# A two-layer mixture-of-experts kernel behind a scan: w1 copies of the units past the scan move to VectorE, router logits stay on the chip, one more weight staging buffer, zeroing spread over steps, and a lighter early weight schedule

## The chip, the core and the metric

The kernel runs on one core of a Trainium2 chip. The metric is the device time of one launch in microseconds (us); lower is better. TensorE (PE) multiplies matrices, VectorE (DVE), ScalarE (ACT) and GpSimd (POOL) do the elementwise work, and SyncE (SP) issues most of the transfers, in program order on one queue. GpSimd issues the transfers whose target rows come from an index list (scatters).

## The reference

`x` and `f_logit` have shape (4, 5056, 256). A gated recurrence runs along the sequence, and its output, 20224 rows of 256, goes through two mixture-of-experts layers with 8 experts each (256 to 1024 to 256). The first layer is applied only to rows with a positive skip score and adds its result to the row; the second is applied to all rows and replaces them.

```python
f = lower_bound + (1 - lower_bound) * sigmoid(f_logit)
h = f[:, t] * h + (1 - f[:, t]) * x[:, t]        # for every t; y[:, t] = h

# layer 1 (rows with x @ w_skip > 0), layer 2 (all rows, without the "x +")
e = argmax(x @ w_gate); g = softmax(x @ w_gate)[e]
out = x + g * (relu(x @ w1[e]) @ w2[e])
```

## The kernel before, in words

**Regions.** DRAM holds a buffer `regions` with one stretch of rows for each expert of each layer. A row that has been routed is scattered to the end of its expert's stretch (row of 256 numbers, 8 logits of the second layer, token number, gate; `W` = 272 floats, 1088 bytes). A *unit* is 256 rows (or 128, for what is left over) of one expert, read back as one block.

**Steps.** Units have numbers u = 0 to 125. A unit has four steps; step k = 4u + f. In step k, `Moe.step` first stores what the unit before has finished (`put1`), then issues the first product of quarter f (`mm1`, line 604: 12 matmuls, so 48 for a unit), then the work ahead (`ahead`): at f = 3 the load of unit u + 2 (`load`, line 559), at f = 0 the copy of w1 for unit u + 1 (`stage`, lines 568 to 578), at f = 2 the transposes of unit u + 1 (`xpose`, line 591). Then follows the second product of the step two before (`mm2`, lines 632 to 634), the end of a unit (`finish1` or `finish2`), and the side work (`side`). The order of the instructions on every engine is the order of this text.

**Stages.** Sixteen iterations of the scan run before step 0, with the splitting of the first layer's weights into two float16 halves (`weights`, `wload`, `wsplit`; 4 quarters for each of 8 experts, 32 calls in all; `WI`, `WS` and `WD` say in which steps of which iteration a call is made). Units 0 to 27 run beside the rest of the scan, one iteration (512 rows) for each unit. Units 28 to 41 are the rest of layer 1: 28 to 31 and 32, 34, 36, 38, 40, 41 have 256 rows, 33, 35, 37, 39 have 128. Units 42 to 125 are layer 2, the last six of 128 rows. Units 0 to 7 and 42 to 49 have a known expert and read w1 in place in the weight store `wt`. For the others the expert is only known on the chip, and 1024 KB of w1 are copied to a fixed place: in layer 1 by a transfer on SP's queue (line 575, `wt<-wt` for units 8 to 27, `w1s<-wt` for 28 to 41), in layer 2 by a VectorE copy (line 578).

**From layer 1 to layer 2.** Finished layer-1 rows can't be scattered at once, since their places depend on counts. `put1` writes a unit's rows to a DRAM buffer `mid` (line 651) and their logits, 32 bytes for each row, to a DRAM buffer `midl` (line 653). After the scan, three sorts (`sort_later`, `sorting`; 52, 12 and 16 tiles of 128 rows) read the logits back (line 1258) and compute target rows and gates on VectorE. Then `sort_some` sends one pair of tiles for each step: SP reads it from `mid` into one of 7 or 8 slots in the weight store (line 1336), three steps later ScalarE writes the gates (line 1327) and GpSimd scatters the two tiles (line 272). The third sort starts at step 172. The lists of layer 2 are made from step 4 * 42 + 12 = 180 on; they are needed by the load of unit 50 in step 195.

**Buffers.** Blocks of rows have three buffers, so the load of unit u + 2 waits until what unit u - 1 stored has landed. The staging buffers `wst` (two) take the quarters of the second layer's weights (`weights2`: each call first splits the quarter of two calls ago, then loads the next, lines 1127 and 1130) and, once, a block of zeros `zr2`, which `zero2` writes behind the last row of each expert of layer 2: 8 transfers (lines 783 to 785), issued by the list generator, of which `listing` takes up to 5 pieces in one step.

Of the kernel before, what the change touches and what calls it, by code (L numbers as in the profile page):

```python
# [8 lines left out]
F32 = mybir.dt.float32  # L9
# [8 lines left out]
P = 128  # L18
B, S, D, E, F = 4, 5056, 256, 8, 1024
NT = B * S  # L20
# [5 lines left out]
UT = 256  # L26
UJ = UT // P
CP = NT + 2 * UT
NREG = 2 * E
LR = E // 2 * CP + UT  # L30
# [4 lines left out]
I0, LN, NEARLY, K1A, K1B = 16, 4, 8, 6, 4  # L35
K2E, K2A, K2B = 8, 70, 6
NFIX = E // LN
NMID = LN * NEARLY * UJ + K1A * UJ + K1B
GC = GT // CJ


DL, DB, UF, KL = 2, 3, 5, 12

WQ = [(e, k) for e in range(E) for k in (2, 3)] + [(e, k) for e in range(E) for k in (0, 1)]
WI, WS, WD = [1, 2] * 8, [1, 3], 1
WL = 17
WT = 24
LG, LB, LA1 = 4, 3, 1
# [10 lines left out]
CLG, CTOK, CGATE = D, D + E, D + E + 1  # L59
# [33 lines left out]
def moe_chain(ctx: ExitStack, tc: tile.TileContext, xT, fT, lb, wg, w1a, w2a, w1b, w2b, out):  # L93
    nc = tc.nc
# [4 lines left out]
    regf = reg[:]  # L99
# [188 lines left out]
    lists = ctx.enter_context(tc.tile_pool(name="lists", bufs=1))  # L288

    midt = tc.dram_tile([NMID * P, W], F32, name="mid")  # L290
    mid = midt[:]
    midl = tc.dram_tile([P, NMID, E], F32, name="midl")[:]
    vals = lists.tile([P, NMID], F32, name="vals")

    def region(name):
# [239 lines left out]
    class Moe:  # L535


        def __init__(m, pools, w1s):
            m.w1s = w1s
            m.xp, m.hp, m.px, m.pm, m.po, m.pr = pools  # L540
            m.t, m.put = {}, None

# [23 lines left out]
        def stage(m, u):  # L566

            t = m.t[u]
            if t.lo == t.hi:
                t.w1 = wt[:, t.lo : t.lo + W2O]  # L570
                return
            t.w1 = m.w1s(u)
            if not t.L.l2:
                o = nc.sync.value_load(t.L.reg[0:1, 1, t.ur], min_val=t.lo, max_val=t.hi)
                nc.sync.dma_start(t.w1, wt[:, bass.ds(o, W2O)])
            else:
                o = nc.vector.value_load(t.L.reg[0:1, 1, t.ur], min_val=t.lo, max_val=t.hi)
                nc.vector.tensor_copy(t.w1, wt[:, bass.ds(o, W2O)])  # L578
# [68 lines left out]

        def put1(m):
            t, m.put = m.put, None
            r0 = (t.L.tiles + t.at * t.uj) * P  # L650
            nc.sync.dma_start(mid[r0 : r0 + t.ut, :].rearrange("(j p) w -> p j w", p=P), t.rows)
            j0 = r0 // P
            nc.sync.dma_start(midl[:, j0 : j0 + t.uj, :], t.rows[:, :, CLG : CLG + E])

        def send1(m, u):

# [73 lines left out]
    with ExitStack() as ph:  # L730
# [4 lines left out]
        mp = ph.enter_context(tc.tile_pool(name="mp", bufs=2))  # L735
        hp = ph.enter_context(tc.tile_pool(name="hp", bufs=3))
        ul = ph.enter_context(tc.tile_pool(name="ul", bufs=1))
        late = K()

        def w1s1(u):  # L740

            if u < U1:
                o = E * ES + u % 2 * W2O
                return wt[:, o : o + W2O]
            return w1s2(u)
# [3 lines left out]

        U1 = nchunk + 3 - I0 + 1  # L750
        pools = (mp, hp, pt, pm, po, pr)
        moe, tail = Moe(pools, w1s1), Moe(pools, w1s2)

        ap_ = ph.enter_context(ExitStack())
        xp_ = ap_.enter_context(tc.tile_pool(name="ldx", bufs=3))
# [15 lines left out]
        def zero2(pool):  # L771

            zs = pool.tile([P, E], F32, name="zs")
            nc.vector.tensor_tensor(out=zs, in0=S2.c0, in1=sgn8, op=ALU.mult)
            yield
            at = pool.tile([1, E], I32, name="at")
            nc.vector.tensor_tensor(out=at, in0=zs[0:1, :], in1=blk8[0:1, :], op=ALU.add)
            yield
            z = late.s.tile([P, F], F32, tag="wst", name="zr2")[:, : UJ * W].rearrange("p (j w) -> p j w", w=W)
            nc.gpsimd.memset(z, 0.0)  # L780
            for e in range(E):
                r0 = e // 2 * CP + e % 2 * (CP - UT - NT)
                r = nc.sync.value_load(at[0:1, e : e + 1], min_val=r0, max_val=r0 + NT)
                dst = regf[bass.ds(r + LR, UT), :].rearrange("(j p) w -> p j w", p=P)
                r = nc.sync.dma_start(dst, z)
                for g in ("scat", "ld1", "zero"):
                    tc.declare_no_dep(r.ins, group=g, reason="rows without tokens, of one expert")
                tc.add_to_no_dep_group("zero", r.ins)
                yield

        C = {}
        Q = {}
# [432 lines left out]
        DG = K()  # L1225
        DG.todo, DG.now, DG.send, DG.held, DG.n = [], None, [], [], 0

        def sort_later(k):
            last = [None] * NMID
            for u, (L, at) in enumerate(units):  # L1230
                uj = L.ut // P
                for j in range(uj):
                    last[L.tiles + at * uj + j] = u
            a = LN * NEARLY * UJ
            t0 = max(t for t in range(a) if 4 * last[t] + 6 <= k)
            t0 += t0 % 2
            for t0, t1 in ((0, t0), (t0, a), (a, NMID)):
                DG.todo.append((t0, t1 - t0, max(last[t0:t1])))
            DG.most = max(n for _, n, _ in DG.todo)

            late.past = late.d.tile([P, P], F16, name="past")
            nc.vector.tensor_scalar(out=late.past, in0=ltri, scalar1=-1.0, scalar2=None, op0=ALU.add)

        def sorting(t0, n, c):

            v = nc.vector
            shp = [P, n, E]
            m = DG.most

            def tile3(name, dt=F32):  # L1250
                t = late.d.tile([P, m * E], dt, name=name)
                return t[:, : n * E].rearrange("p (n e) -> p n e", e=E)

            def tile1(name, dt=F32, bufs=1):
                return late.d.tile([P, m], dt, name=name, bufs=bufs)[:, :n]

            lg = tile3("b_lg")
            nc.sync.dma_start(lg, midl[:, t0 : t0 + n, :])

            on = late.d.tile([P, m * E], F16, name="b_on")[:, : n * E]  # L1260
            nc.gpsimd.memset(on, 1.0)
            nc.gpsimd.memset(on.rearrange("p (e n) -> p e n", e=E)[:, :, 0], 0.0)
            yield
            yield
            mx = tile1("b_mx")
            v.tensor_reduce(out=mx, in_=lg, op=ALU.max, axis=AX.X)
            v.tensor_tensor(out=lg, in0=lg, in1=mx.unsqueeze(2).broadcast_to(shp), op=ALU.subtract)
# [126 lines left out]
        n1 = LN * NEARLY + K1A + K1B  # L1394
        n = n1 + K2E + K2A + K2B
        q2 = iter(range(4, 4 * E + 2))

        def side(k):
# [8 lines left out]
            if s == CS:  # L1407
                e, r = divmod(i - (I0 - CK), LN)
                if r == 0 and 0 <= e < NEARLY:
                    lists_of_scan(e)  # L1410
            if s == 3 and i == nchunk + 2:
                for _ in G[2]:
                    pass
                ap_.close()
                late.w = ph.enter_context(tc.tile_pool(name="w1s", bufs=WB))
                late.s = ph.enter_context(tc.tile_pool(name="wst", bufs=2))
                late.l = ph.enter_context(tc.tile_pool(name="lists2", bufs=1))
                late.d = ph.enter_context(tc.tile_pool(name="small2", bufs=1))
                lists_after_scan()
                sort_later(k)  # L1420
# [4 lines left out]
            if k == 4 * n1 + KL:  # L1425
                assert not GL.todo and DG.counted == NMID
                lists_of_layer2()
                assert len(units) == n
            if i > nchunk + 2:
                listing(LT if k < 4 * n1 else LT2, True, 3)  # L1430
                sort_some(k)
            else:
                listing(max(GL.n, 1), s in PS, LA)
            if i < I0:
# [7 lines left out]
            u = i - I0 - n1  # L1442
# [52 lines left out]
```

## Time and profile before

| what | value |
|---|---|
| median of 3 runs | 1603.25 us (1598.87 to 1607.89) |
| the profiled execution's own time | 1619.11 us |
| its span, first to last instruction | 1617.4 us |
| PE busy | 1506.5 us (93%) |
| DVE, ACT, POOL busy | 904.6, 719.7, 499.6 us |
| mean granted TensorE clock | 0.975 |

Durations and waits come from the one profiled execution, which is 15.9 us above the median of the runs. The clock is the share of full speed (2.4 GHz) that was granted; the other level is 1.2 GHz, so 0.83 in a stretch means that it was at the lower level for a third of it. The DMA share is the mean busy share of 16 DMA engines.

### The profile page before, as it was taken

The page shows a single profiled execution, that of the slowest core. Times are in us where ns is not written, and L with a number is a line of the kernel's source. Part 1 is how long each engine was busy: PE and PEld are TensorE (multiplying, and loading weights), DVE is VectorE, ACT ScalarE, POOL GpSimd, SP SyncE. Part 2 cuts the span into 40 slices and gives each one's busy share as a digit, 9 for nine tenths or more (in the row PEclk, how much of TensorE's full clock was granted, in tenths as well). Part 3 has the DMA queues.
Part 4 walks back from the last instruction along what each step waited for, and adds up shares of the span by engine and source line. Part 5 has one row for each costly group of instructions (what it writes and reads, how often), then busy time and mean ns, then how long its engine had stood idle before and what let it go on. Part 6 is the DMA issues. An engine that isn't in the chain of part 4 may idle for free.

```text
span 1617.4 us, 41213 instructions
## 1 busy us (share of the span) xinstructions
PE 1506.5 (93%) x13897; PEld 1343.9 (83%) x13898; DVE 904.6 (56%) x1915; ACT 719.7 (44%) x1376; POOL 499.6 (31%) x509
## 2 busy tenths in 40 slices
PE   6877999999999977898899999999999999999996
PEld 5776888888887866787689999989989998998996
DVE  5887687878775633445575555544444444444443
ACT  6885667666662221333344444433333333333332
POOL 1663556454643265113311111111111111111111
PEclk9987999999999999999999999999999999999998
DMA  8876647777754689616333332211111111111110
GB/s 290 278 262 215 224 167 246 245 247 235 251 195 168 193 277 298 219 51 209 115 100 96 100 107 88 88 54 54 46 51 55 48 48 55 48 50 52 55 42 26
DMA packets 138998, 228.56 MB, mean 141 GB/s; under 512 B 24571, under 2 KB 97791, under 8 KB 134448
## 3 DMA queue, kind: packets, MB, share of 16 engines
q1 hardware_dynamic: 119600, 172.33, 33.5%
q0 software_dynamic: 19200, 53.53, 9.1%
q8 instruction: 132, 2.16, 0.6%
q14 instruction: 66, 0.54, 0.1%
HBM read 120.16 MB, written 70.86 MB: 118 GB/s over the span
## 4 chain that ended last, share of the span: by engine, by line
PE 80%; DMA 6%; DVE 5%; issue 4%; ACT 3%; SPq 1%; POOL 1%; another core or an unknown queue 1%; POOLq 0%; ACTq 0%; DVEq 0%
PE ps_m L604 36%; PE ps_o L632 12%; PE ps_o L633 12%; PE ps_o L634 12%; PE ps_x L591 3%; DVE xt L838 1%; PE ps_t L862 1%; DMA rows<-regions 1%; DMA ft<-in_fT_dram 1%; DMA wt<-mid 1%; PE ps_l L890 1%; DMA midl<-rows 1%; PE ps_v L1019 1%; DMA regions<-rw,dest 1%; ACT hh L615 1%
## 5 line engine op out<-in xcount | busy, mean ns | idle before, releaser
L616 DVE SCALAR_TENSOR_TENSOR hl<-ps_m,hh 128x512 f16<-128x512 f32 (+1 forms) x504 | 336.8, 669 | 595.5 <-ACT hh L615 574.1
L615 ACT ACTIVATE hh<-ps_m 128x512 f16<-128x512 f32 (+1 forms) x504 | 292.3, 580 | 704.2 <-PE ps_m L604 522.2
L632 PE MATMUL ps_o<-wt,hh 128*128 (+2 forms) x1936 | 532.9, 275 | 6.7 <-DVE rows L640 4.2
L634 PE MATMUL ps_o<-wt,hl 128*128 (+2 forms) x1936 | 532.5, 275 | 2.5 <-issue 2.5
L633 PE MATMUL ps_o<-wt,hh 128*128 (+2 forms) x1936 | 532.7, 275 | 0.6 <-issue 0.6
L604 PE MATMUL ps_m<-xh,w1s 128*128 128x256 f16 (+1 forms) x2880 | 509.1, 268 | 8.5 <-issue 3.6
L604 PEld LDWEIGHTS <-w1s 128*128 128x128 f16 x4320 | 407.1, 98 | 60.2 <-issue 10.6
L272 POOL DMA_INDIRECT out_dram<-rows,dest x162 | 157.8, 974 | 751.9 <-ACT rows L669 687.1
L604 PE MATMUL ps_m<-xl,w1s 128*128 128x256 f16 (+1 forms) x1440 | 379.6, 268 | 1.7 <-issue 1.4
L604 PE MATMUL ps_m<-xh,wt 128*128 128x256 f16 x1152 | 216.9, 276 | 4.6 <-issue 4.5
L633 PEld LDWEIGHTS <-hh 128*128 128x128 f16 x1936 | 190.5, 98 | 33.1 <-issue 8.6
L634 PEld LDWEIGHTS <-hl 128*128 128x128 f16 x1936 | 190.4, 98 | 27.8 <-issue 2.5
L632 PEld LDWEIGHTS <-hh 128*128 128x128 f16 x1936 | 190.5, 98 | 23.5 <-issue 0.7
L272 POOL DMA_INDIRECT regions<-rw,dest x158 | 173.3, 1097 | 84.5 <-issue 50.0
L604 PEld LDWEIGHTS <-wt 128*128 128x128 f16 x1728 | 168.4, 99 | 30.8 <-issue 10.5
L604 PE MATMUL ps_m<-xl,wt 128*128 128x256 f16 x576 | 158.8, 276 | 2.4 <-issue 2.1
L272 POOL DMA_INDIRECT regions<-wt,b_dest x80 | 78.8, 984 | 99.6 <-ACT wt L1327 58.3
L578 DVE COPY w1s<-wt 128x4096 f16 x76 | 93.3, 1228 | 8.5 <-issue 2.1
L838 DVE TENSOR_TENSOR_SCAN xt<-ft,end,xt 128x512 f32<-128x512 f32 (+4 forms) x78 | 95.0, 1248 | 0.3
L591 PE MATMUL ps_x<-ident,rows 128*128 128x128 f32 x484 | 75.3, 277 | 19.7 <-DMA rows<-regions 15.0
L593 DVE SCALAR_TENSOR_TENSOR xl<-ps_x,xh 128x512 f16<-128x512 f32 (+1 forms) x126 | 83.3, 661 | 10.0 <-ACT xh L592 9.9
L669 ACT ACTIVATE rows<-ps_o,rows 128x256 f32<-128x256 f32 x162 | 68.6, 473 | 32.7 <-PE ps_o L634 32.3
(231 smaller groups left out, 1298.8 us busy)
## 6 DMA issues: line engine op xcount, KB each, us to landing
rows<-regions SPq DMA_DIRECT2D x116, 272.0 KB
wt<-wt SPq DMA_DIRECT2D x20, 1024.0 KB
ft<-in_fT_dram SPq DMA_DIRECT2D x39, 512.0 KB
xt<-in_xT_dram SPq DMA_DIRECT2D x39, 512.0 KB
w1s<-wt SPq DMA_DIRECT2D x14, 1024.0 KB
wt<-mid SPq DMA_DIRECT2D x40, 272.0 KB
mid<-rows SPq DMA_DIRECT2D x38, 272.0 KB
wt<-in_w2a_dram SPq DMA_DIRECT2D x16, 512.0 KB
```

Of the source, the lines that this page charges most:

```text
L272: r = nc.gpsimd.indirect_dma_start(out=dst, out_offset=bass.IndirectOffsetOnAxis(ap=idx_ap, axis=0), in_=rows_ap, in_offset=None, bounds_c ...
L578: nc.vector.tensor_copy(t.w1, wt[:, bass.ds(o, W2O)])
L591: nc.tensor.transpose(ps[:, d, j * P : (j + 1) * P], t.rows[:, j, d * P : (d + 1) * P], ident)
L593: nc.vector.scalar_tensor_tensor(out=t.xl, in0=ps, scalar=SX, in1=t.xh, op0=ALU.mult, op1=ALU.subtract)
L604: nc.tensor.matmul(ps[:, f, :], lhsT=t.w1[:, wo : wo + P], rhs=x[:, d, :], start=f == 0 and k == 0, stop=f == 1 and k == 5, skip_group_che ...
L615: nc.scalar.activation(hh, ps, AF.Relu)
L616: nc.vector.scalar_tensor_tensor(out=hl, in0=ps, scalar=0.0, in1=hh, op0=ALU.max, op1=ALU.subtract)
L632: nc.tensor.matmul(ps, lhsT=hh[:, f, js], rhs=hi, start=first, stop=False)
L633: nc.tensor.matmul(ps, lhsT=hh[:, f, js], rhs=lo, start=False, stop=False)
L634: nc.tensor.matmul(ps, lhsT=hl[:, f, js], rhs=hi, start=False, stop=last)
L669: nc.scalar.activation(y, t.ps[j][:, :D], AF.Copy, scale=t.rows[:, j, CGATE : CGATE + 1])
L838: nc.vector.tensor_tensor_scan(x[:, d, s0:s1], f[:, d, s0:s1], x[:, d, s0:s1], init, ALU.mult, ALU.subtract)
```

## The change

- Layer-1 units from 28 on (`u >= U1`) copy w1 with VectorE instead of a transfer on SP's queue.
- Logits are gathered on the chip by a ScalarE copy in `put1`. For scan units they go to `midl` once for four units (256 bytes for each partition); for units 32 to 41 they stay in a tile `late.lg`, which the last sort reads in place, without a transfer and two steps sooner.
- The sorts are cut into pieces of at most `NB` = 24 tiles: 24, 24, 16 and 16 tiles instead of 52, 12 and 16.
- The staging pool `wst` gets a third buffer.
- The 8 zero transfers are put in a list, and one is issued in each step.
- The lists of layer 2 start one step earlier (`KL` 11).
- Of the 32 weight calls, 21 instead of 24 are made in the first 16 scan iterations; the others follow from iteration 16 (step 0) on instead of 17.

```diff
+NSCAN = LN * NEARLY * UJ
+NMID = NSCAN + K1A * UJ + K1B
+NB = 24
-DL, DB, UF, KL = 2, 3, 5, 12
+DL, DB, UF, KL = 2, 3, 5, 11
-WI, WS, WD = [1, 2] * 8, [1, 3], 1
+WI, WS, WD = [1, 2, 1] * 5 + [1], [1, 3], 0
...
-    midl = tc.dram_tile([P, NMID, E], F32, name="midl")[:]
+    midl = tc.dram_tile([P, NSCAN, E], F32, name="midl")[:]
+    lgs = lists.tile([P, LN * UJ, E], F32, name="lgs")
...
-            if not t.L.l2:
+            if u < m.by_dma:
                 o = nc.sync.value_load(t.L.reg[0:1, 1, t.ur], min_val=t.lo, max_val=t.hi)
                 nc.sync.dma_start(t.w1, wt[:, bass.ds(o, W2O)])
             else:
...
         def put1(m):
             t, m.put = m.put, None
+            j0 = t.L.tiles + t.at * t.uj
+            if j0 >= NSCAN:
+                nc.scalar.copy(late.lg[:, j0 - NSCAN : j0 - NSCAN + t.uj, :], t.rows[:, :, CLG : CLG + E])
+            else:
+                j = j0 % (LN * UJ)
+                nc.scalar.copy(lgs[:, j : j + t.uj, :], t.rows[:, :, CLG : CLG + E])
+                if j + t.uj == LN * UJ:
+                    nc.sync.dma_start(midl[:, j0 - j : j0 - j + LN * UJ, :], lgs)
             r0 = (t.L.tiles + t.at * t.uj) * P
             nc.sync.dma_start(mid[r0 : r0 + t.ut, :].rearrange("(j p) w -> p j w", p=P), t.rows)
-            j0 = r0 // P
-            nc.sync.dma_start(midl[:, j0 : j0 + t.uj, :], t.rows[:, :, CLG : CLG + E])
...
-        moe, tail = Moe(pools, w1s1), Moe(pools, w1s2)
+        moe, tail = Moe(pools, w1s1, U1), Moe(pools, w1s2, 0)
...
             nc.gpsimd.memset(z, 0.0)
+            yield
             for e in range(E):
-                r0 = e // 2 * CP + e % 2 * (CP - UT - NT)
-                ...
-                yield
+                ZG.append((z, at, e))
+        ZG = []
+        def zero_one():
+            if not ZG:
+                return
+            z, at, e = ZG.pop(0)
+            ...            # the same register load and transfer as before, for one expert
...
-            t0 = max(t for t in range(a) if 4 * last[t] + 6 <= k)
-            t0 += t0 % 2
-            for t0, t1 in ((0, t0), (t0, a), (a, NMID)):
+            t0 = max(t for t in range(0, NSCAN, LN * UJ) if 4 * max(last[:t], default=0) + 6 <= k)
+            cuts = sorted({*range(0, t0, NB), *range(t0, NSCAN, NB), NSCAN, NMID})
+            for t0, t1 in zip(cuts[:-1], cuts[1:]):
                 DG.todo.append((t0, t1 - t0, max(last[t0:t1])))
+            late.lg = late.d.tile([P, NMID - NSCAN, E], F32, name="lg")
...
-            lg = tile3("b_lg")
-            nc.sync.dma_start(lg, midl[:, t0 : t0 + n, :])
+            if c:
+                lg = late.lg
+            else:
+                lg = tile3("b_lg")
+                nc.sync.dma_start(lg, midl[:, t0 : t0 + n, :])
...
-            yield
-            yield
+            if not c:
+                yield
+                yield
...
-                late.s = ph.enter_context(tc.tile_pool(name="wst", bufs=2))
+                late.s = ph.enter_context(tc.tile_pool(name="wst", bufs=3))
...
                 sort_some(k)
+                zero_one()
```

## Rows read from the trace of the kernel before

**Rows 1.** Windows: stretch, length; busy PE, PEld, DVE, ACT, POOL; clock, DMA share, GB/s.
```profile
261.00:510.00 249.00, 239.44 (x2403) 212.21 (x2402) 191.72 (x489) 156.70 (x293) 125.12 (x111) 1.00 0.69 231
525.00:695.00 170.00, 146.85 (x1315) 123.52 (x1313) 78.07 (x217) 43.90 (x108) 63.03 (x68) 0.96 0.73 239
695.00:750.00 55.00, 55.00 (x506) 49.37 (x505) 25.40 (x72) 18.41 (x38) 7.64 (x16) 1.00 0.27 85
...
791.00:1567.00 776.00, 776.00 (x7105) 698.33 (x7103) 371.56 (x605) 286.80 (x521) 138.33 (x142) 1.00 0.21 66
```

**Rows 2.** Windows of line 604's matmuls alone, 48 to a unit; clock, DMA share.
```profile
525.00:572.00 47.00, 23.70 (x192) 1.00 0.66 218
572.00:673.00 101.00, 41.92 (x387) 0.93 0.82 268
673.00:695.00 22.00, 11.68 (x97) 1.00 0.48 153
...
750.00:791.00 41.00, 14.19 (x97) 0.83 0.60 197
...
1567.00:1604.00 37.00, 20.00 (x288) 1.00 0.12 37
```

**Rows 3.** Waits of SP's queue, whole run: total us, times, longest us.
```profile
SPq L559 <- DMA midl<-rows: 51.6, 29, 6.6
...
SPq L559 <- DMA mid<-rows: 16.9, 7, 5.5
```

**Rows 4.** Chain that ended last, 640 to 690: start us, us, what.
```profile
669.83 6.63 DMA midl<-rows
676.48 2.71 DMA rows<-regions
```

**Rows 5.** Waits of PE, stretch 525 to 695: total us, times, longest us.
```profile
PE ps_x L591 <- DMA rows<-regions: 6.5, 5, 2.6
PE ps_m L604 <- issue: 5.0, 9, 1.0
...
PE ps_m L604 <- DMA w1s<-wt: 2.5, 2, 1.5
```

**Rows 6.** Line 272 in the stretch 525 to 673: ns min/median/max, first and last start.
```profile
L272 POOL DMA_INDIRECT regions<-wt,b_dest x64: 968/975/978, 551.5 to 656.6; - x64
```

**Rows 7.** Timeline of SP, stretch 690 to 800: start us, us, instruction.
```profile
742.59 3.87 SPq L785 DMA_DIRECT2D regions<-zr  x4
...
749.53 5.24 SPq L785 DMA_DIRECT2D regions<-zr  x4
...
759.71 0.39 SPq L559 DMA_DIRECT2D rows<-regions  x1
```

**Rows 8.** Timelines of PE and POOL, 756 to 784; idle time before in brackets.
```profile
763.69 1.11 PE L591 MATMUL ps_x<-ident,rows 128*128 128x128 f32 x4 [7.14 <-DMA rows<-regions]
...
777.34 0.27 PE L604 MATMUL ps_m<-xl,wt 128*128 128x256 f16 x1 [1.14 <-issue]
...
762.50 0.98 POOL L272 DMA_INDIRECT regions<-wt,b_dest  x1 [0.30 <-issue]
```

**Rows 9.** Waits of SP's queue, stretch 735 to 800.
```profile
SPq L1127 <- DVE wt L183: 13.4, 2, 8.8
```

**Rows 10.** Groups by line: count, busy us, mean ns.
```profile
L578 DVE COPY w1s<-wt 128x4096 f16 x76 | 93.3, 1228 | 8.5 <-issue 2.1 <-DMA wst<-in_w1b_dram 1.2
...
L183 DVE SCALAR_TENSOR_TENSOR wt<-wt 128x1024 f16<-128x1024 f32 x24 | 29.4, 1227 | 18.1 <-ACT wt L182 16.8 <-issue 1.1
...
L920 ACT COPY lg<-ls 128x32 f32<-128x32 f32 (+1 forms) x40 | 8.7, 216 | 0.0
```

**Rows 11.** Timeline of DVE, scan before the units: one line 826 an iteration.
```profile
59.02 1.23 DVE L826 SCALAR_TENSOR_TENSOR xt<-ft,xt 128x1024 f32<-128x1024 f32 x1 [0.93 <-ACT rw L865]
...
67.36 1.22 DVE L826 SCALAR_TENSOR_TENSOR xt<-ft,xt 128x1024 f32<-128x1024 f32 x1
...
76.53 1.23 DVE L826 SCALAR_TENSOR_TENSOR xt<-ft,xt 128x1024 f32<-128x1024 f32 x1 [0.94 <-ACT ft L821]
```

More of the change, by code (lines that the diff above doesn't have):

```diff
@@ L37 @@
 NFIX = E // LN
-NMID = LN * NEARLY * UJ + K1A * UJ + K1B
+NSCAN = LN * NEARLY * UJ
+NMID = NSCAN + K1A * UJ + K1B
+NB = 24
 GC = GT // CJ
-DL, DB, UF, KL = 2, 3, 5, 12
+DL, DB, UF, KL = 2, 3, 5, 11
 WQ = [(e, k) for e in range(E) for k in (2, 3)] + [(e, k) for e in range(E) for k in (0, 1)]
-WI, WS, WD = [1, 2] * 8, [1, 3], 1
+WI, WS, WD = [1, 2, 1] * 5 + [1], [1, 3], 0
 WL = 17
@@ L291, in moe_chain @@
     mid = midt[:]
-    midl = tc.dram_tile([P, NMID, E], F32, name="midl")[:]
+    midl = tc.dram_tile([P, NSCAN, E], F32, name="midl")[:]
+    lgs = lists.tile([P, LN * UJ, E], F32, name="lgs")
+    late = K()
     vals = lists.tile([P, NMID], F32, name="vals")
@@ L535, in moe_chain, with __init__ @@
     class Moe:
-        def __init__(m, pools, w1s):
-            m.w1s = w1s
+        def __init__(m, pools, w1s, by_dma):
+            m.w1s, m.by_dma = w1s, by_dma
             m.xp, m.hp, m.px, m.pm, m.po, m.pr = pools
@@ L737, in moe_chain @@
         ul = ph.enter_context(tc.tile_pool(name="ul", bufs=1))
-        late = K()
         def w1s1(u):
@@ L780, in zero2 @@
             nc.gpsimd.memset(z, 0.0)
+            yield
             for e in range(E):
-                r0 = e // 2 * CP + e % 2 * (CP - UT - NT)
[L783 to L788, printed above, removed]
-                yield
+                ZG.append((z, at, e))
[4 more added lines that the diff above has]
+            z, at, e = ZG.pop(0)
+            r0 = e // 2 * CP + e % 2 * (CP - UT - NT)
+            r = nc.sync.value_load(at[0:1, e : e + 1], min_val=r0, max_val=r0 + NT)
+            dst = regf[bass.ds(r + LR, UT), :].rearrange("(j p) w -> p j w", p=P)
+            r = nc.sync.dma_start(dst, z)
+            for g in ("scat", "ld1", "zero"):
+                tc.declare_no_dep(r.ins, group=g, reason="rows without tokens, of one expert")
+            tc.add_to_no_dep_group("zero", r.ins)
         C = {}
@@ L1233, in sort_later @@
                     last[L.tiles + at * uj + j] = u
-            a = LN * NEARLY * UJ
-            t0 = max(t for t in range(a) if 4 * last[t] + 6 <= k)
-            t0 += t0 % 2
-            for t0, t1 in ((0, t0), (t0, a), (a, NMID)):
+            t0 = max(t for t in range(0, NSCAN, LN * UJ) if 4 * max(last[:t], default=0) + 6 <= k)
+            cuts = sorted({*range(0, t0, NB), *range(t0, NSCAN, NB), NSCAN, NMID})
+            for t0, t1 in zip(cuts[:-1], cuts[1:]):
                 DG.todo.append((t0, t1 - t0, max(last[t0:t1])))
-            DG.most = max(n for _, n, _ in DG.todo)
+            late.lg = late.d.tile([P, NMID - NSCAN, E], F32, name="lg")
             late.past = late.d.tile([P, P], F16, name="past")
@@ L1247, in sorting @@
             shp = [P, n, E]
-            m = DG.most
+            m = NB
             def tile3(name, dt=F32):
@@ L1428, in side @@
                 assert len(units) == n
+            if k == 4 * (n1 + K2E - 2) + 3:
+                assert not ZG and not DG.send and not DG.held and DG.now is None
             if i > nchunk + 2:
```

## The prediction

> **What bounds the kernel now.** I read the windows by stage first. Past 791 us TensorE is busy 776.00 of 776 us at full clock, and from 695 to 750 it is busy 55.00 of 55 [rows 1]: in layer 2 nothing but TensorE's own work sets the time, so the change can win nothing there. In the scan stage (261 to 510) TensorE is busy 239 of 249. The stage with room is 525 to 695, units 28 to 41: 147 of 170, clock 0.96, DMA share 0.73.
>
> The windows of the first product alone turn this into units [rows 2]. 673 to 695 holds 97 matmuls, two units, so a unit of 256 rows takes 10.9 us when nothing is late; 1567 to 1604 holds six units of 128 rows in 37 us, 6.2 each. Against these paces:
>
> - 525 to 572: four units in 47 us instead of 43.6, 3.4 lost.
> - 572 to 673: four large and four small units in 101 us instead of 68.4, 32.6 lost.
> - 750 to 791: two units in 41 us instead of 21.8, 19.2 lost.
>
> Then I ask what was late. In the first two stretches TensorE waits for blocks of rows (6.5 us), for w1 transfers (2.5) and for "issue", where the profile names nothing (5.0 for the first product) [rows 5]; the rest is lower clock after each wait (0.93) and waits further back. The chain of waits shows the pattern: the small transfer of logits lands 6.63 us after its issue, only then may the next block be loaded, 2.71 us more [rows 4]. SP's queue says the same over the run: 29 loads waited for logits, 7 for the rows beside them [rows 3]. In the third stretch the load of unit 48, due in step 187, goes out at 759.71, behind eight zero transfers that begin at 742.59 and end at 754.77 [rows 7] and behind a weight load that waited for a split, up to 8.8 us [rows 9]. TensorE stands 7.14 us for it, and later crawls one matmul at a time [rows 8], while GpSimd runs sixteen scatters back to back.
>
> **The change, part by part.**
>
> *Copies and logits, 525 to 695.* Fourteen transfers of 1024 KB go, with the logits' transfers of these units. In their place come fourteen VectorE copies of 1.23 us [rows 10], 17 us on an engine that is busy 78 of 170, and ScalarE copies of about 0.2 us (nearest row: 216 ns for 32 numbers a partition). A copy stands at the start of a unit, ahead of the halves that the second product needs two steps later; layer 2 runs so at full pace, large units and small [rows 1, 2], so I cost it at nothing while that cover of two steps holds.
>
> What is late next? First the row store: a load then waits for `mid` instead of `midl`. From the store to the transposes there are four steps: 10.9 us in large units, about 8.6 across a large and a small one. Before, 6.63 + 2.71 = 9.3 us had to fit. The row store is issued ahead of the logits and was seldom the last [rows 3], so it should fit, with less margin in small units. Then GpSimd: 64 scatters of 0.975 us lie between 551.5 and 656.6 [rows 6], with 0.30 between neighbours [rows 8], so they need 81.6 of these 105.1 us, and this train can shrink by 23.5 us at most. No copy lies in that stretch before the change; some nine would lie in it after. If a copy and a scatter exclude each other, the train needs 81.6 + 9 x 1.23 = 92.7 us and shrinks by 12.4.
>
> No row shows the two together. The Trainium skill (SBUF — State Buffer, Who interferes with whom) says that a VectorE copy in a two-port mode and GpSimd's work on a scatter block each other for a whole instruction; by this the term would be 12 us and not 21, and no run here shows it yet.
>
> TensorE need not follow GpSimd step by step, since seven slots stand between. Lower bound of the gain: the waits that the rows name, 6.5 + 2.5 = 9 us. Upper: 23.5 for the train, the 3.4 before it and some 3 after it, 30 us. I take 21, nearer to the train's limit, because the transfers that go are the largest in the stretch.
>
> *Zeros, third buffer, earlier last sort, 750 to 791.* One zero transfer then takes about 1 to 1.3 us of SP in a step of 2.7 us, so SP is no longer twelve microseconds behind, and a weight load does not wait until the zero block has landed. The last sort ends two steps earlier, so its scatters don't fall together with late loads; the earlier lists have the same effect. The load of unit 48 should go out near 748 us. One flaw: the zero block now keeps a buffer through eight steps (183 to 190), so the weight load of step 188 has two buffers left and still waits for a split [rows 9]; the load of unit 49 three steps later covers most of that. Lower bound: the 7.14 us wait plus about 1 us of low clock, 8; upper: 19.2. I take 17, with the crawl gone, since it stands beside the bunched scatters.
>
> *Cut sorts.* Four instead of three, with shorter operands; some 5 us more on a VectorE with 90 us to spare. Steps 118 to 150 send the same 32 pairs. Nothing.
>
> *Weights.* Ahead of the units an iteration with one call takes 8.34 us and one with two 9.17 [rows 11], 0.83 for a call, so three fewer give 2.5 (bounds 0 and 3.7, three splits of 1.23 on VectorE [rows 10]). They come back in units 0 to 6, between 0 and 3.7; TensorE has little room there, and I take 1.
>
> *Logit copies beside the scan.* 28 more ScalarE instructions of 0.2 us, 0 to 6 us; SP has 28 small transfers to issue less. ScalarE is busy 157 of 249 [rows 1], and I take 1.
>
> **The sum.** 21 + 17 + 2.5 - 1 - 1 = 38.5 us less. Against the profiled execution, 1619.1, this gives 1580.6. That execution is 15.9 us above the median of the runs, and where these lie is not told. If they lie outside the stretches that gain, the median falls by all of 38.5, to 1564.7; if all lie in them, by 22.6, to 1580.6. I take a point between, a fall of 32 us: 1571 us.
>
> **The rivals.**
>
> - *GpSimd paces units 29 to 38*, because copies and scatters exclude each other. For: the train is at 78% of its stretch already. Against: layer 2 has both and keeps its pace, though only two scatters to a unit. The first term is 12 instead of 21; 29.5 in all, in the median about 25: 1578 to 1579, and 1585 if the "issue" waits grow with it.
> - *Unit 48 or 49 is late again*, because the zero block holds a buffer and SP waits for splits. For: 13.4 us of such waits [rows 9]. Against: the three steps of cover. The second term is 8; 29.5 in all: 1579.
> - *It does not do what it says*: the row store of 272 KB, on the same queue, ends the waits as late as the logits did. For: loads waited for it 7 times, 16.9 us, more than 2 us each [rows 3]. Then the first term is 3, the second 8, the scan stage gives back 5: 6 less, 1597.
> - *Slower*: in `put1` ScalarE now waits for `finish1` on VectorE, in every scan unit, with the next relu queued behind it, then its low half on VectorE, then the second product. For: VectorE is busy 192 of 249 us there and often late. Against: two steps of cover. The other terms win about 32 in the median, so it decides from 32/28 = 1.1 us a unit; at 1.7 us the time is 1619.
>
> **How the numbers follow.** Forecast 0.52 (1571, its own range 1562 to 1580), GpSimd's pace 0.17, unit 48 late 0.13, no effect 0.10, slower 0.08. What a measurement of this kernel can tell from no change is about 0.5%, 8 us: 1595 to 1611. The first three cases are faster, 0.82; the no-effect case 0.10; slower 0.08. The range reaches from 1556, where nearly all losses go (55 us in the profile, at the share of 32 to 38.5 some 46 to 47 in the median), to 1594, and leaves out the last two cases.
>
> **What would show it.** Right: in the stage of units 28 to 41 the DMA share falls below 0.65, waits for `midl` vanish from SP's list, and 572 to 673 holds its eight units in some 80 us; units 47 and 48 take under 24 us together, with one zero transfer in a step. GpSimd's rival shows as scatters longer than 0.98 us or copies longer than 1.23, and as SP waiting for a slot of line 1336; the slower one as ScalarE waiting for `finish1` and scan units above their pace; the no-effect one as loads waiting for `mid`. The prediction is wrong if TensorE's lost time in 525 to 695 stays above 25 us.

## The result, and the profile after

The changed kernel takes 1585.9 us (median of 4 runs, 1576.8 to 1587.3) beside 1605.0 us for the kernel before (4 runs, 1598.9 to 1607.9): a ratio of 0.987, 95% interval 0.983 to 0.992, 19 us less. The forecast was 1571, so the direction was right and the size too large. The profiled execution of the change took 1587.3 us with a span of 1585.6, close to its median; that of before had taken 1619.1, far above its own.

The windows by stage of the changed kernel, in the columns of [rows 1], with the stage of units 47 to 49 added (727 to 767):

```profile
261.00:510.00 249.00, 245.65 (x2489) 219.45 (x2487) 196.77 (x504) 165.85 (x322) 133.87 (x116) 1.00 0.69 238
522.00:672.00 150.00, 138.39 (x1315) 121.42 (x1314) 96.70 (x255) 46.78 (x124) 69.46 (x70) 0.99 0.58 181
...
727.00:767.00 40.00, 36.28 (x314) 31.43 (x312) 24.51 (x74) 16.50 (x30) 18.04 (x17) 0.96 0.64 211
767.00:1536.00 769.00, 769.00 (x7053) 692.11 (x7051) 364.69 (x575) 282.76 (x516) 136.16 (x140) 1.00 0.21 65
```

Units 28 to 41 take 150 us where they took 170 [rows 1], at a DMA share of 0.58 instead of 0.73. Layer 2 is TensorE's own work, as before. The first product alone (line 609 now) over the same units as [rows 2]:

```profile
522.00:569.00 47.00, 23.86 (x195) 19.05 (x196) 1.00 0.49 151
569.00:651.00 82.00, 37.00 (x383) 30.81 (x381) 0.98 0.70 224
651.00:672.00 21.00, 11.91 (x96) 9.39 (x96) 1.00 0.30 84
727.00:756.00 29.00, 12.83 (x98) 10.18 (x99) 0.94 0.77 254
```

The eight units from 32 to 39 fell from 101 to 82 us, units 47 and 48 from 41 to 28; the first four of the stretch hardly moved (47.3 to 46.1). What is late now? The waits of SP's queue from 510 to 672, and under them the one wait of any size that TensorE has from 522 to 672:

```profile
SPq L564 <- DMA regions<-wt,b_dest: 44.7, 8, 7.6
...
SPq L564 <- DMA mid<-rows: 9.8, 7, 2.4
```
```profile
PE ps_x L596 <- DMA rows<-regions: 11.3, 7, 2.7
```

No load waits for `midl` any more, and those for `mid` are short in this stretch. (Over the whole run the wait changed its name more than its size: 83.9 us for `mid` in 33 waits, where the kernel before has 96.1 in e9, 68.7 for `midl` and 27.4 for `mid`.) But eight row loads wait up to 7.6 us for a scatter of the sorts, which write rows counted later than the unit's, and TensorE stands 11.3 us for the loads.

### The profile page after: what moved, and what is told of

It is laid out like the page before. It is cut to its first block, busy times and chain, and to the rows that moved or that the text cites. A ratio compares the mean times of both kernels' runs of the same rounds, so it can differ in the third digit from the quotient of the medians.

```text
span 1585.6 us, 41240 instructions
## 1 busy us (share of the span) xinstructions
PE 1498.6 (95%) x13900; PEld 1346.4 (85%) x13901; DVE 925.5 (58%) x1947; ACT 725.0 (46%) x1419; POOL 507.9 (32%) x511
## 5 line engine op out<-in xcount | busy, mean ns | idle before, releaser
L583 DVE COPY w1s<-wt 128x4096 f16 x90 | 110.8, 1231 | 11.6 <-issue 4.8
L274 POOL DMA_INDIRECT regions<-wt,b_dest x80 | 84.7, 1059 | 42.2 <-issue 17.9
L598 DVE SCALAR_TENSOR_TENSOR xl<-ps_x,xh 128x512 f16<-128x512 f32 (+1 forms) x126 | 83.1, 660 | 16.7 <-ACT xh L597 16.6
```

Source lines behind the costliest of these rows:

```text
L274: r = nc.gpsimd.indirect_dma_start(out=dst, out_offset=bass.IndirectOffsetOnAxis(ap=idx_ap, axis=0), in_=rows_ap, in_offset=None, bounds_c ...
L598: nc.vector.scalar_tensor_tensor(out=t.xl, in0=ps, scalar=SX, in1=t.xh, op0=ALU.mult, op1=ALU.subtract)
```

## The experiments

The table is worked out from the traces: the start of each unit's first product (48 matmuls to a unit of line 604 or 609), as lengths in us from the start of the first unit named to the start of the one after the last. The last column is TensorE's idle time put down to "issue", for which the profile names no cause.

```
kernel                    start  0-7    8-27  28-31 32-39  40-41 47-48  span    issue
before                    143.4  117.5  264.3  47.3 100.3  22.1  41.1  1617.4   22.2
change                    140.4  126.6  255.6  46.1  82.4  21.5  28.1  1585.6    0
e5 before                 151.7  122.9  267.0  47.4 101.2  22.3  40.3  1633.5   18.3
e6 change                 147.2  116.1  266.8  49.0  94.8  21.2  28.9  1606.4   24.5
e9 before                 150.8  117.0  254.4  46.3  98.1  22.2  32.8  1605.0    0
e1 free loads             143.0  122.4  255.6  46.1  76.6  21.4  29.1  1576.9    0
e10 free loads            145.5  125.1  255.7  46.1  76.2  21.4  30.3  1583.7    0
e2 weights as before      142.5  118.8  256.1  46.1  86.8  20.9  29.6  1583.1    0
e3 logits as before       141.3  121.8  255.4  46.0  85.9  22.0  28.5  1582.9    0
e4 zeros as before        144.7  120.1  255.6  46.1  85.9  22.4  33.0  1590.7    0
e7 w1 by transfers        143.7  118.9  266.2  47.7 101.2  21.3  30.3  1611.7   20.4
e8 free, old weights      149.5  125.0  270.1  48.3  95.6  21.2  26.1  1625.0   23.0
e11 free, ScalarE copies  146.1  116.1  254.2  47.8  78.9  23.1  29.9  1578.8    0
e12 free, no GpSimd split 144.2  114.3  255.8  46.1  74.5  21.4  30.2  1569.2    0
```

The experiments ran on three chips, with the kernel before timed beside them on each: e1 to e4 on one (before: 1601.5 us), e5 to e8 on a second (1631.9) and e9 to e12 on a third (1603.8). For the first profiles of before and change no chip is on record.

**Which profile of before to compare with (e5, e6, e9).** The two first profiles differ in units 8 to 27 too, by 8.7 us, where no part of the change would save time. So both kernels were profiled again unchanged.

> The kernel before, unchanged, for a second profile. Theory A: the profiled execution that the prediction used was a slow one (1619 against a median near 1603); its 22 us of TensorE waits named issue and part of the loss of units 47 and 48 belong to that execution. Then this profile is 10 to 18 us shorter, has under 8 us of issue waits, units 8 to 27 take 255 to 259 us instead of 264 and units 47 and 48 under 36 instead of 41. Rival B: the waits belong to the kernel, and this profile repeats them within 3 us in each stage.

> The changed kernel, unchanged, beside the others on the same chip: a second profile and a narrower interval, expected at 0.988 (0.985 to 0.991) of the kernel before. Its stages should repeat within 3 us, units 0 to 7 within 5.

> The kernel before, profiled once more beside kernels with the change. In two profiles of it TensorE stood 22 and 18 us for nothing that the profile shows, and units 8 to 27, whose code the change leaves alone, took 264 and 267 us; in the profiles of the change on the first chip that idle time is 0 and these units take 255.5. Theory (this belongs to the chip or its condition, not to the kernel): where the three kernels below show no such idle time, this one shows none either, its units 8 to 27 take 255 to 257 us, its units 32 to 39 about 88 to 96 and its span is 1595 to 1608. Rival (the change itself takes that time away): 262 us or more in units 8 to 27 and 15 us or more of such idle time here, and none in the kernels below.

e5: 1635.2 us. e6: 1614.5, ratio 0.991 (0.988 to 0.994). e9: 1606.7. TensorE's waits for "issue" over the whole run of e6, whose code shows none in the first profile of the change:

```profile
PE ps_m L609 <- issue: 12.7, 15, 2.5
...
PE ps_o L637 <- issue: 5.5, 6, 1.9
```

Both kernels have them in some executions and not in others, 18 to 25 us or 0, and with them units 8 to 27 take 264 to 270 us, without them 254 to 256. It is not the change. All four profiles of the second chip have them, and none of the eight of the other two, so e5 came out against its theory: the waits repeat there. The profile on which the prediction rests had them, that of the change had not. e9 is the like one: it takes 1605.0 of span, 19.4 above the change, and 1606.7 in time, 2.9 above its chip's median of before. Its windows of units 28 to 41 and of 47 and 48, then the first product of units 32 to 39, then TensorE's and SP's waits in the first of these stretches:

```profile
522.00:689.00 167.00, 144.31 (x1316) 123.97 (x1314) 80.23 (x223) 45.31 (x108) 63.02 (x68) 0.96 0.75 245
...
744.00:778.00 34.00, 26.54 (x216) 22.58 (x214) 18.48 (x72) 11.46 (x22) 22.63 (x22) 0.85 0.72 235
```
```profile
569.00:667.00 98.00, 38.98 (x386) 32.14 (x384) 0.93 0.84 275
```
```profile
PE ps_x L591 <- DMA rows<-regions: 17.3, 7, 4.7
PE ps_m L604 <- DMA w1s<-wt: 5.2, 6, 1.3
```
```profile
SPq L559 <- DMA midl<-rows: 21.7, 13, 4.8
...
SPq L559 <- DMA regions<-wt,b_dest: 6.6, 5, 2.9
```

Like with like, e9 to the change: units 28 to 41 fall from 166.6 to 150.0 us, 16.6 less; units 47 and 48 by 4.7; start and units 0 to 7 together by 0.8, which the spread hides (below); units 8 to 27 rise by 1.2, the rest by 1.5. That is the whole 19.4. The two profiles are of two chips. The wait for scatters was there before, 6.6 us, behind the larger one for `midl`.

**Row loads freed from later scatters (e1, e10).** A load of one of the last ten first-layer units (32 to 41; the expectation of e10 says 14) reads rows that were in place before the sorts, yet it is ordered behind the newest scatter. `Moe.load` already drops that order for units of lists that hold only full ones (8 to 31); the edit drops it here as well:

```
-            if L.full:
+            if L.full or (not L.l2 and isinstance(at, int) and L.row is None):
```

> The changed kernel, but the row loads of units 32 to 41 are declared independent of scatters counted after their list was made (layer-2 rows, which they never read). Theory A: in the changed kernel these loads waited for the newest scatter of the sorts (44.7 us in 8 waits on SP between 510 and 672), so GpSimd's train set the pace of units 32 to 39. Then those waits vanish, TensorE's 11.3 us of waits for rows in that stretch fall below 4, units 28 to 41 take 140 us or less instead of 150, and the time is 7 to 11 us below the changed kernel, about 0.981 of the kernel before. Rival B (the transfers themselves are slow under load, the scatter wait ends at the same moment as the wait for the stored rows): the waits move to mid<-rows or to a slot of the send, and the time stays within 3 us of the changed kernel, 0.986 to 0.989. Rival C (GpSimd and VectorE exclude each other and hold VectorE): no change in the stretch either, scatters beside copies stay at 1.4 to 1.8 us.

> The change, with the row loads of the last 14 first-layer units freed from the scatters that bring rows counted later. Theory (those loads end last in units 32 to 41 only while nothing else slows TensorE there): on a chip where TensorE shows no idle time without a visible cause, units 32 to 39 take 75 to 79 us again and the ratio is 0.983 to 0.989; on one that shows it, they take 88 to 96 and the ratio is 0.987 to 0.993. Rival (the first run of it was lucky): 82 to 87 us on a chip without such idle time.

e1: 1580.0 us, ratio 0.987 (0.984 to 0.989). e10: 1575.3, 0.981 (0.979 to 0.984). In both profiles units 32 to 39 take 76 to 77 us where the change has 82.4 and e2 to e4, which keep the order, 86 to 87. SP's waits from 510 to 672 and TensorE's from 526 to 670 in e10:

```profile
SPq L1358 <- DMA regions<-wt,b_dest: 19.8, 13, 4.3
SPq L564 <- DMA mid<-rows: 16.5, 13, 4.4
```
```profile
PE ps_x L596 <- DMA rows<-regions: 4.2, 5, 1.3
```

The wait of 44.7 us is gone. What SP waits for now is a slot that a scatter still reads (line 1358), and TensorE's wait for rows is 4.2 us instead of 11.3 (5.8 in e1, where under 4 was expected). The two intervals of the same code do not overlap, if barely, so a ratio differs from chip to chip by more than its interval says, here by 0.005. The change itself was not timed on these two chips. Its own median lies 6 and 11 us above e1's and e10's, by the ratios 1 and 10; on the chip of e1, e3 and e2, which are the change with one small part undone, are 5.0 and 7.0 us slower than e1. That fits the stage's 6 us. On the chip with "issue" waits e8, which has the edit too, shows 95.6 us beside e6's 94.8: no gain there.

**Copies: what they bought, and what they cost (e7, e11).** e7 sends w1 of units 28 to 41 by transfers again, with everything else of the change kept; e11 is e10 with these copies on ScalarE.

```
-        moe, tail = Moe(pools, w1s1, U1), Moe(pools, w1s2, 0)
+        moe, tail = Moe(pools, w1s1, LN * NEARLY + K1A + K1B), Moe(pools, w1s2, 0)      (e7)

-                o = nc.vector.value_load(t.L.reg[0:1, 1, t.ur], min_val=t.lo, max_val=t.hi)
-                nc.vector.tensor_copy(t.w1, wt[:, bass.ds(o, W2O)])
+                eng, cp = (nc.vector, nc.vector.tensor_copy) if t.L.l2 else (nc.scalar, nc.scalar.copy)
+                o = eng.value_load(t.L.reg[0:1, 1, t.ur], min_val=t.lo, max_val=t.hi)   (e11)
+                cp(t.w1, wt[:, bass.ds(o, W2O)])
```

> The changed kernel, but units 28 to 41 take w1 by the 1024 KB transfers again. Theory A (these transfers were the main load of the stretch): the DMA share there rises from 0.58 to above 0.68, units 28 to 39 take 136 to 145 us instead of 128, and the time rises by 8 to 15 us, 0.993 to 0.998 of the kernel before. Rival B (the scatters paced the loads in any case, and without VectorE copies the train of 64 scatters is some 5 us shorter): units 28 to 39 within 3 us of 128, the time within 3 us of the changed kernel or below it.

> As the kernel above, with the copies of w1 in units 28 to 41 on ScalarE in place of VectorE (those of the second layer stay on VectorE). Theory (a VectorE copy and a GpSimd scatter that meet hold each other up, 10 or 11 scatters of 1.4 to 1.8 us in place of 0.97, some 6 us of the train of 64): with ScalarE's copies no scatter among the 64 lasts over 1.1 us but for those that meet other VectorE work, the train takes 83 to 86 us in place of 90, and where that train is the limit units 32 to 39 gain 0 to 5 us against the kernel above. Rival (the long scatters wait for something else, such as their descriptors' way to memory): as many of 1.4 us and more as before. A loss is possible where a copy on ScalarE takes longer than the 1.23 us on VectorE and comes ahead of the hidden rows of the unit at hand: 14 units by about 1 us.

e7: 1613.3 us, 0.990 (0.987 to 0.993), beside e6's 1614.5. Its units 32 to 39 take 101.2 us and e6's 94.8, so the transfers cost 6 us there by the two profiles, but the times are the same: on that chip the gain of the copies is not to be seen in the time. e6's profile is also the fastest of its six executions, 1608.2 us against their median of 1614.5, so its 94.8 may be low.

e11: 1580.3 us, 0.985 (0.983 to 0.988), not better than e10. It does settle whether copies and scatters meet. In the change the first scatter of the train, the copy that falls on it, and the next scatter, in the timelines of POOL and DVE:

```profile
548.54 1.79 POOL L274 DMA_INDIRECT regions<-wt,b_dest  x1 [11.22 <-DMA rows<-regions]
550.63 0.97 POOL L274 DMA_INDIRECT regions<-wt,b_dest  x1 [0.30 <-issue]
```
```profile
548.98 1.23 DVE L583 COPY w1s<-wt 128x4096 f16 x1
```

The scatter ends 0.12 us after the copy. Later the two meet in both ways, again POOL and DVE:

```profile
590.50 0.98 POOL L274 DMA_INDIRECT regions<-wt,b_dest  x1 [0.30 <-issue]
591.79 1.58 POOL L274 DMA_INDIRECT regions<-wt,b_dest  x1 [0.30 <-issue]
```
```profile
591.09 1.44 DVE L583 COPY w1s<-wt 128x4096 f16 x1
```

The first scatter, 0.59 us ahead of the copy, keeps its 0.98 us and the copy takes 1.44 instead of 1.23; the second starts inside the copy and ends 0.84 us after it. Of the 64 scatters, 11 overlap a copy and take 1.44 us on average (up to 1.81); the other 53 take 0.97. Eight of the 11 are held, and each of these ends 0.12 or 0.84 us after its copy; the other three started 0.59 to 0.74 us ahead of theirs, were not held, and stretched the copy to 1.28 to 1.44 us. The groups of the 64 scatters, in e10 and in e11, and e11's copies:

```profile
L274 POOL DMA_INDIRECT regions<-wt,b_dest x64 | 68.9, 1076 | 31.9 <-issue 14.3 <-DMA rows<-regions 11.2 <-ACT wt L1349 3.4
```
```profile
L584 ACT COPY w1s<-wt 128x4096 f16 x13 | 46.9, 3606 | 2.9 <-issue 1.7 <-DMA regions<-wt,b_dest 0.7
...
L274 POOL DMA_INDIRECT regions<-wt,b_dest x64 | 62.6, 978 | 37.3 <-ACT wt L1350 19.9 <-issue 14.6 <-ACT hh L621 2.1
```

With ScalarE copying, 23 scatters overlap a copy and none lasts over 1.12 us: the long ones were VectorE's doing, and cost 6.3 us in 64. The train falls from 90.9 to 85.3 us and no further, because ScalarE, 3.61 us in each copy, writes the gates late (19.9 us of GpSimd's waits). TensorE gains nothing from it: units 32 to 39 take 78.9 us where e10 has 76.2, and the rest of the stage 3.4 more. Since ScalarE's longer copies cost something themselves, what a shorter train alone is worth is not shown.

**The other parts undone one at a time (e2, e3, e4, e8).** e2 takes back the weights' calls, e3 the logits on chip (each unit sends its own to `midl`, and every sort loads them), e4 the third buffer and the spread zeros; e8 joins e1's edit and e2's.

```
-WI, WS, WD = [1, 2, 1] * 5 + [1], [1, 3], 0                           (e2, e8)
+WI, WS, WD = [1, 2] * 8, [1, 3], 1

+            j0 = r0 // P                                              (e3)
+            nc.sync.dma_start(midl[:, j0 : j0 + t.uj, :], t.rows[:, :, CLG : CLG + E])

                 ZG.append((z, at, e))                                 (e4)
+                zero_one()
+                yield
...
-                late.s = ph.enter_context(tc.tile_pool(name="wst", bufs=3))
+                late.s = ph.enter_context(tc.tile_pool(name="wst", bufs=2))
```

> The changed kernel with the weight calls of the kernel before (24 in the first 16 iterations, the rest from iteration 17). Theory A: moving three calls into units 0 to 6 costs more than it saved, since ScalarE, VectorE and GpSimd are full there: unit 0 starts 3 us later again (143 instead of 140), units 0 to 7 take 117 us instead of 127, and the time falls by 4 to 7 us, to about 0.984 of the kernel before. Rival B (the longer units 3 and 5 come from something else in the change, the ScalarE copies that wait for finish1, or are chance): units 0 to 7 stay near 126 us and the time rises by 2 to 4 us, about 0.989.

> The changed kernel with the logits sent to midl by one small transfer for each unit again, and read back by all four sorts. Theory A: beside the scan the small transfers cost little, past it a load waits for them (up to 6.6 us before the change); with the large w1 transfers gone they land in some 3 us, and the loads of units 32 to 41 wait for scatters anyway, so 1 to 4 us are lost, about 0.989. Rival B (the shorter odd units between 9 and 25, 8.7 us in all, are due to the logits staying on the chip): units 8 to 27 take 264 us instead of 255.6 and the time rises by 8 us or more, 0.992 or above.

> The changed kernel with two staging buffers and with the eight zero transfers issued by the list generator in two steps again; the earlier lists and last sort stay. Theory A (the zeros' burst on SP's queue held the load of unit 48): units 47 and 48 take 38 us or more instead of 28, the load of unit 48 goes out over 8 us later against its unit, and the time rises by 9 to 13 us, about 0.995. Rival B (the earlier end of the last sort did it): units 47 and 48 stay under 31 us and the time within 3 us, 0.986 to 0.989.

> The changed kernel with both edits: loads of units 32 to 41 independent of the sorts' scatters, and the weight calls of the kernel before. If the weight shift really cost something (units 0 to 7 at 118.8 us with the old calls against 120 to 127 with the new), the time is 2 to 5 us below the first edit alone, about 0.984; if it is even (unit 0 starts 2 us later, the units take 2 to 4 us less), it is within 2 us of it, 0.986 to 0.988.

e2: 1587.0 us, 0.990 (0.988 to 0.993). e3: 1585.0, 0.990 (0.988 to 0.993). e4: 1589.3, 0.992 (0.990 to 0.995). e8: 1620.5, 0.993 (0.991 to 0.996).

Weights: unit 8 starts (start and units 0 to 7 added) between 261 and 275 us with the old calls (five profiles, mean 268) and between 262 and 271 with the new (eight, without e12; mean 265): 3 us in favour of the new, less than the spread of either. Chip by chip it looks different. On the one with "issue" waits the old calls have 274.6 and 274.5 us (e5, e8) and the new 263.4 and 262.6 (e6, e7), 11 us, and e8, expected at 0.984 to 0.988, is 6 us slower than e6 in time; on the other two, 267.8 and 261.3 (e9, e2) stand among the 262 to 271 of the new. With two profiles a side, and e8 holding a second edit, that is a hint and no proof. Logits: 85.9 us in units 32 to 39 beside the 82.4 of the change, and the same time; no share of the gain can be told to be theirs once the large transfers are gone. With the small transfers back but the large ones gone, loads wait 8.9 us for `midl` from 510 to 690, where e9 has 21.7.

Zeros: units 47 and 48 take 33.0 us, as in e9, and not the 38 or more that was expected. In e4, TensorE's one long wait from 729 to 774, then POOL's timeline and SP's ahead of it:

```profile
PE ps_x L596 <- DMA rows<-regions: 7.1, 1, 7.1
```
```profile
726.07 0.97 POOL L274 DMA_INDIRECT regions<-wt,b_dest  x1 [6.46 <-DMA regions<-zr]
...
734.55 0.98 POOL L274 DMA_INDIRECT regions<-wt,b_dest  x1 [6.23 <-DMA regions<-zr]
735.83 0.97 POOL L274 DMA_INDIRECT regions<-wt,b_dest  x1 [0.30 <-DVE hl L621]
737.11 1.02 POOL L274 DMA_INDIRECT out_dram<-rows,dest  x1 [0.31 <-issue]
```
```profile
724.98 5.04 SPq L806 DMA_DIRECT2D regions<-zr  x5
...
741.25 0.39 SPq L564 DMA_DIRECT2D rows<-regions  x1
```

Zeros in a burst land late, and the last sort's scatters wait twice for them, 6.46 and 6.23 us. The output scatters of an earlier unit stand behind in GpSimd's queue, at 737.11, and the load of unit 48 waits until they have freed its rows buffer. In the profiles of before it is SP that stands behind the burst [rows 7]; the end is the same, 7.1 us of TensorE [rows 8]. Spread zeros and third buffer give 4.9 us against the change, and 2.7 to 4.9 against all the profiles without "issue" waits that have them (28.1 to 30.3 us); the earlier lists and the earlier last sort give nothing by themselves. What is left in the change, 28.1 us instead of 21.8, in its timelines of SP, POOL and ScalarE:

```profile
733.70 0.39 SPq L564 DMA_DIRECT2D rows<-regions  x1
...
748.48 0.40 SPq L564 DMA_DIRECT2D rows<-regions  x1
```
```profile
725.45 0.97 POOL L274 DMA_INDIRECT out_dram<-rows,dest  x1 [0.30 <-issue]
...
742.49 0.97 POOL L274 DMA_INDIRECT out_dram<-rows,dest  x1 [0.31 <-ACT hh L620]
743.77 0.97 POOL L274 DMA_INDIRECT out_dram<-rows,dest  x1 [0.30 <-issue]
```
```profile
721.86 0.84 ACT L681 ACTIVATE rows<-ps_o,rows 128x256 f32<-128x256 f32 x2 [0.39 <-PE ps_o L639]
...
732.78 0.84 ACT L681 ACTIVATE rows<-ps_o,rows 128x256 f32<-128x256 f32 x2 [0.39 <-PE ps_o L639]
```

The loads of units 48 and 49 wait for a rows buffer too, 5.4 and 3.4 us. For unit 49 it is the queue: the output rows of unit 46 are ready at 733.62 and their scatters begin at 742.49, 8.9 us later, behind the sort's. For unit 48 it is more the landing: the rows of unit 45 are ready at 722.70, their two scatters begin 2.8 us later and land 5.6 and 6.7 us after issue, where the first of those at 742.49 takes 2.4. A fourth rows buffer was not tried.

**GpSimd's splits (e12).** Some small VectorE operations last far over their usual 0.17 us beside a split on GpSimd. In the changed kernel, the timelines of DVE and POOL:

```profile
227.28 2.85 DVE L435 TENSOR_SCALAR us<-us 128x8 f32<-128x8 f32 x1
```
```profile
227.96 2.14 POOL L191 TENSOR_TENSOR wt<-wt 128x1024 f16<-128x1024 f32 x1
```

All such lengthening, over the median of the same instruction, adds up to 27 us in that profile, 10 of it beside these splits and 16 beside another GpSimd operation of the scan (line 893), which the experiment leaves in place. e12 is e10 without any split of weights on GpSimd (eight of 32 weight blocks have one).

```
-WT = 24
+WT = 32
```

> As the second kernel, with the splits of weights that GpSimd does up to unit 24 left to the other engines until step 32, that is, none of them on GpSimd. Theory (VectorE's small operations of 0.17 us that last up to 2.85 beside a GpSimd operation of 2.14 cost the units up to 7 some of their time, 23 to 28 us of lengthening in all): units 0 to 7 fall from 117 to 127 us to 110 to 118, and the time by 2 to 8 us. Rival (those operations are off the path, and what GpSimd did now loads VectorE and ScalarE): units 0 to 7 as before or longer by up to 5 us, the time the same or longer.

e12: 1573.1 us, 0.982 (0.979 to 0.984), the same as e10. In its profile the lengthening falls to 20 us and units 0 to 7 take 114.3 us, fewer than in any other; e10's took 125.1. But e11, with the splits, has 116.1, and over the timed runs none of that is left: no gain can be put down to the splits, and what moves these units between 114 and 127 us is not known.

## Why the prediction was right, and where its sizes were off

**The bound and the parts that gain: right.** Units 28 to 41 and units 47 and 48 are where time was lost and where it came from; layer 2 gave nothing. The waits for `midl` vanished, the DMA share fell below 0.65, the eight units went to 82 us (forecast "some 80"), and TensorE's lost time in units 28 to 41 is 150 - 133.8 = 16 us, under the 25 that would have refuted it.

**The zeros, sized 17, gave 4.7: the step that failed most.** It took nearly all that the profile of before showed over pace, 19.2 us, as something the zeros, the buffer and the lists set. In e9 these units lose 32.8 - 21.8 = 11.0. The other 8 stood in one kind of execution alone; the "issue" waits that [rows 8] shows among the crawl were the sign of it, and I had put the crawl down to the bunched scatters. And 6.3 us of loss stayed, by a wait that I had not named: a rows buffer that output scatters free, begun 8.9 us late behind the sort's in GpSimd's queue or landing as late as 6.7 us after issue. On the chip with "issue" waits the same stretch does fall further, from 40.3 to 28.9 us. "Under 24" was wrong on every chip. The rival of a late unit 48 is what came, at 4.7 where it said 8, but for another reason than the held buffer. The 13.4 us that I cited for it were misread, too: the waits for a split [rows 9] lie after the load of unit 48 has gone out, at 777 to 791 us; ahead of that load SP's weight load waited 2.9 us, for zeros to land.

**Units 28 to 41, sized 21, gave 16.6.** The step that failed is "TensorE need not follow GpSimd step by step, since seven slots stand between". It does follow: not by the slots, but because a row load waits for the newest scatter. With that order dropped the stage takes 144.1 and 143.7 us, 22.5 to 22.9 less than e9: the term was right for a kernel without it. Taking the first wait away (6.63 us for `midl` in [rows 4]) brought the second one out, 6.6 us in e9 and 44.7 in the change.

**GpSimd's rival: half right.** The train of 64 scatters shrank from e9's 102.4 us to 89.9, by 12.5 where this rival gave 12.4, and scatters over 0.98 us are there. On this the Trainium skill (SBUF — State Buffer, Who interferes with whom) points the right way: a VectorE copy in a two-port mode and GpSimd's work on a scatter block each other. The trace agrees in kind: eight of 11 scatters are held until their copy is over, and three copies are lengthened by a scatter ahead of them. The term was still too large, 0.47 us for each of 11 meetings instead of nine times 1.23, since the two overlap only in part; and which of them starts first does not decide, as six scatters that began 0.06 to 0.47 us ahead of the copy were held all the same. But the train as such does not pace the units: e1's and e10's trains are as long as the change's (90.3 and 90.9 us), and their units 6 us faster.

**Small terms.** The weights' 2.5 less 1 agree with 3 us of means within a spread of 10, and on one chip the profiles say 11; nothing can be told. The scan stage's cost for logit copies is 1.2 us at most, from 254.4 to 255.6, so ScalarE's wait for `finish1` costs next to nothing and the slower rival falls. The no-effect rival falls with 9.8 us of waits for `mid` past the scan; beside the scan its sign is there, the loads wait for `mid` instead of `midl`, and units 8 to 27 keep their 254 to 256 us.

**From the profile to the median.** I scaled a sum of 38.5 to 32 because the profile lay 15.9 us above the median, not knowing where. It lay in units 8 to 27 (9 to 10 us) and in 47 and 48 (8), with 3 more in units 28 to 41 and 7 less before unit 8. Only 47 and 48 and those 3 were counted as a gain. With the sizes from e9 the sum is 16.6 + 4.7 - 1.2 = 20; measured were 19. That the time still fell into the range is owed to its width, 1556 to 1594, since both large terms were sized too high. The two rivals' terms taken together, 12 and 8, would have made the sum 20.5; I gave each a chance alone and none to both, though their mechanisms were not what came either.

**What stays open.** That the copies made the 16.6 us of units 28 to 41 is argued and not shown. It rests on elimination: with the logits, the weights or the zeros put back, one at a time, the stage still takes 153.8 to 154.4 us against e9's 166.6, which leaves the copies and the cut sorts. The cut sorts were not undone, and the copies only on the chip with "issue" waits, where e7's time did not change. Open too is why the freed loads gain nothing there, and what makes the "issue" waits. Some of the longer ones run into the lower clock: in the profile of before matmuls start 0.11 us apart until 773.1, up to 1.4 apart until 782.3 and 0.21 apart behind that; which of the two brings the other, no run tells.

## What to carry to other kernels

When the profiled execution lies above the median, look for the idle time without a cause and for stages that run over their own pace where nothing is late, and take these losses out before a term is sized by them. When the longest wait of a stage is removed, read in the same list who waited second for the same instruction: the loads here already waited for scatters whose rows they never read. An order against rows that are not read can hide while another wait covers it, and shows its cost only after.

## What the hardware did that was not expected

- The same kernel took 1601 to 1605 us on some chips and 1632 on another, with 0 us of TensorE idle time without a visible cause in the profile of one of the former (e9) and 18 in that of the latter (e5); the ratio of the change moved less, 0.987 and 0.991.
- A copy of 128x4096 16-bit numbers takes 1.23 us on VectorE and 3.61 on ScalarE; of the two only VectorE's holds up a scatter (0.97 to 1.44 us on average, 1.81 at most), and it holds it until the copy is over: every held scatter of the change ends 0.12 or 0.84 us after its copy.
- A VectorE operation of 0.17 us took 2.85 beside a GpSimd operation of 2.14, and taking eight such neighbours away, with 8 of 27 us of lengthening, changed no time.
